# State strips in eight array tiles and two PSUM banks, scores in 64x32 tiles, rank updates in 128x32 tiles, and a new written order

## The chip, the core and the metric

The kernel runs on one core of one Trainium2 chip. The metric is the device time of one execution in microseconds (us); lower is better. The kernel before takes 317.76 us, the median of three runs (317.02 to 318.30). Its profiled execution took 317.11 us, of which the trace covers a span of 315.4 us. The engines are named as in the profile: PE is TensorE (its weight loads are PEld), DVE is VectorE, ACT is ScalarE, POOL is GpSimd, and SP issues most of the DMAs.

## The reference

A gated linear attention (4 batches, 8 heads, 768 tokens, 48 features a head) feeds a gated feed-forward layer with a convolution over three tokens:

```python
f = 1 / (1 + exp(-f_logit))
for t in range(S):                                   # S = 768
    state = f[:, :, t, :, None] * state + einsum('bhd,bhe->bhde', k[:, :, t], v[:, :, t])
    y[:, :, t] = einsum('bhd,bhde->bhe', q[:, :, t], state)
x = y.transpose(0, 2, 1, 3).reshape(B, S, H * D)     # H * D = 384
h = maximum(x @ w_in, 0)                             # 384 -> 1024
conv_out = sum over k of conv_w[k] * (h shifted by k - 1 tokens)
out = (h * sigmoid(conv_out)) @ w_out                # 1024 -> 384
```

## The kernel before, in words

The recurrence is computed in 24 chunks of 128 tokens (4 batches of 6), n = 0 to 23. Heads go in four pairs p; the two heads of a pair (j = 0, 1) lie on partitions 0 to 47 and 64 to 111. For a chunk, PE does four kinds of work, each in fp32, so that each matmul stands in the trace as two records (the transposes as one):

- **scores** (`pa`, line 330): eight matmuls of a 48x128 weight, one for each p and j, into a tile of two PSUM banks, bank j. DVE then copies the causal half into `am` (line 332).
- **values** (`py`, line 366): twelve matmuls of the running state `st` with q, and then sixteen of v with `am`, all with 32 output columns. Eight of the twelve are the 48-row "strips" (one array tile of 64 rows by 32 columns); the other four and the sixteen use all 128 rows by 32 columns. The 384 features are cut into twelve groups of 32; group g is written to column strip g % 4 and third g // 4 of one PSUM bank. ACT and DVE evacuate it as a high and a low part into `xT` (lines 393, 395).
- **turned keys** (`ptk`, line 317): four transposes of the scaled keys, evacuated into `kp`.
- **rank updates** (`pk`, line 341): eight matmuls of a 128x64 weight with v (64 columns moved), added into the state by DVE and scaled by POOL (lines 349, 351).

Heads of the pairs p = 2 and 3 are swapped between the two halves of the partitions (`half`, and the layout of the inputs), so that four strips in a row fall on four different column strips:

```python
def half(p, j):
    return 1 - j if p >= NP // 2 else j
```

The feed-forward layer works on eight half batches u of 384 tokens, once the three chunks of a half are in `xT`: `ph` (line 421, 72 matmuls a half) is x @ w_in in three single-pass products of split operands; ACT and DVE do the activation, the convolution and the gate (`hb`, `g`; lines 424 to 442); `gh` and `gl` are the split result (lines 460, 462); `po` (line 474, 24 matmuls for 128 tokens) is the product with w_out. At the start the weights are converted from float64 words by POOL, ACT and DVE (lines 175 to 191), and twelve matmuls `pz` (line 523) that nobody reads are strewn among the first chunks.

PSUM has eight banks: two for `pa` (tag A), one for `py` (tag Y), two for `ptk` and `pk` (tag s, `SB = 2`), three for `ph`, `po`, `pl` and `pz` (tag mm).

The order of the instructions is written by hand: `ORDER` is a list of tokens, each of which advances one generator by a step (`a9` scores of chunk 9, `y9` values, `s9` state, `k9` turned keys, `m2.3` a third of ph of half 2, block 3, `r0.1` part of a po, `w` one pz). Each engine executes its instructions strictly in that order and waits on semaphores where the data or a buffer isn't ready. No scheduler changes it.

Of the kernel before, what the change touches and what calls it, by code (L numbers as in the profile page):

```python
# [9 lines left out]
F32 = mybir.dt.float32  # L10
# [7 lines left out]
P = 128  # L18
# [22 lines left out]
t8 k9 F12 m1.3 m1.4 y7 P6 h1.4 m1.5 m1.4 m0.6 t9 m1.7 m1.5 s7 Q9 m1.6 p10 a8 m1.7 p10 m1.6 P6 m0.6 S1 m1.7 m0.7 y8 P4
j0.6 S2 y8 m1.1 j0.6 s8 y8 P4 m1.2 a9 K10 P7 m1.4 y8 h1.6 P6 k10 m1.2 P7 m1.7 m2.3 k10 s8 m1.6 S1 m1.5 Q10 m2.3 a9
m1.6 m2.2 r0.1 m2.4 s8 r0.0 m2.3 m1.5 m2.4 m1.4 S4 m2.4 m1.3 m2.2 P6 m2.2 m1.3 m1.2 y9 P6 j1.2 y9 M13 m1.5 P7 m1.4 s9
x12 j1.2 s10 V11 a10 L13 S4 m2.3 r0.0 j1.4 m2.5 m2.5 m1.7 G11 m2.5 m2.2 P7 r0.0 P7 P7 r0.0 j1.4 y9 p11 r0.0 r0.1 S6
h2.2 m2.4 p11 S6 r0.1 m1.6 a10 t11 F16 Q11 h2.4 S7 F17 r0.1 V12 y9 t10 S7 r0.1 s9 x12 m1.7 r0.1 K11 s9 r0.0 m1.6 r0.2
G13 m1.0 y10 m2.5 y10 m1.7 p13 m1.0 r0.1 a11 m1.1 r0.0 r0.1 m1.6 M12 m2.7 m1.1 V13 m2.7 K13 F15 j1.6 m2.7 L14 m1.0 L12
m2.0 j1.6 j1.0 V14 m2.0 r0.0 G12 m2.1 h2.6 m2.7 m2.1 m2.1 s10 p12 j1.0 m2.6 p12 m2.0 r0.2 r0.2 y10 m2.6 m2.0 m2.6 r0.2
G14 m2.2 r0.2 m2.4 h2.0 s10 m2.1 r0.2 y10 m2.5 m2.4 p13 r0.2 K12 m2.3 Q13 a11 r0.4 r0.2 m2.6 r0.4 k13 Q12 p14 k12 x15
y11 m2.2 y11 r0.5 t13 a12 m2.3 y11 t12 m2.7 r0.5 r0.4 m2.6 k13 m2.2 m2.0 r0.4 m2.3 m2.0 r0.5 y11 x15 m2.6 r0.5 m2.0
m2.4 m2.1 r0.5 K14 r0.2 m2.5 r0.2 r0.5 m2.1 m2.6 r0.4 j2.2 a12 p14 r0.4 k12 F19 m2.7 M14 G17 y12 L15 F18 s12 y12 m2.1  # L50
F20 r0.5 a13 j2.2 r0.3 m2.7 L16 m3.3 r0.4 m2.5 j2.0 r0.4 m3.2 r0.5 m3.3 h3.2 j2.4 j2.0 V16 m3.1 V15 j2.6 m3.2 y12 M15
s12 m3.2 j2.4 m3.3 m3.1 a13 m3.3 m3.1 m3.2 x18 m3.6 G15 m3.6 m3.7 G16 p15 k14 p15 y13 K15 h3.0 k14 Q15 y13 m3.1 r0.3
# [12 lines left out]
m5.4 K23 m5.6 j4.6 m5.1 m5.4 j4.6 m5.1 h5.0 m5.5 a19 h5.6 k20 m5.1 m5.5 m5.6 r2.1 m5.0 m5.0 m5.6 h5.2 m5.1 y19 m5.5
y19 p22 k21 s20 y19 s21 p22 s20 a20 r2.0 s20 Q22 r2.1 m5.1 m5.7 p23 m5.0 t22 m5.3 m5.0 m5.3 m5.1 t23 m5.3 r2.0 m5.2
m5.2 K22 m5.7 y19 m5.7 a20 m5.2 m5.7 m5.3 y20 m5.2 m5.4 m5.7 y20 m5.1 m5.6 m5.7 a21 y20 m5.4 m5.0 m5.7 r2.1 a21 r2.0
m5.5 m5.0 r2.1 m5.5 m5.0 r2.0 j5.4 s21 j5.0 m5.6 r2.1 m5.6 m5.3 j5.4 r2.1 j5.0 r2.0 r2.2 y20 r2.0 r2.2 y21 r2.0 m5.3
r2.1 y21 j5.6 M23 r2.1 a22 r2.0 V22 a22 k22 m6.6 Q23 m6.4 j5.6 m6.4 m6.6 m6.6 z m6.4 m6.6 m6.1 m5.2 m6.5 h6.4 m6.4
m5.2 m6.5 m6.4 m5.2 m6.1 h6.0 s21 m6.5 m5.3 m6.1 m6.5 m6.7 m6.1 m6.7 h6.6 k22 m6.7 j5.2 m6.2 m6.7 j5.2 m6.2 m6.1 m6.2  # L70
r2.2 m6.5 m6.3 m6.7 m6.0 y21 m6.3 m6.7 m6.2 m6.0 m6.4 r2.3 m6.3 z y21 m6.0 h6.2 r2.3 m6.2 z m6.0 y22 m6.0 m6.4 y22
m6.3 m6.1 r2.2 m6.5 s22 y22 m6.0 m6.3 a23 m6.6 m6.6 r2.3 m6.7 r2.2 m6.6 m6.3 r2.2 m6.1 m6.5 r2.2 a23 r2.2 m6.2 m6.0
r2.3 r2.5 s22 r2.3 r2.5 r2.3 m6.2 s22 r2.5 y22 r2.3 r2.2 r2.3 j6.4 y23 r2.2 j6.6 y23 j6.6 r2.5 y23 j6.0 j6.4 r2.5 r2.4
j6.0 r2.5 y23 h7.0 m6.3 m7.1 j6.2 m7.0 r2.5 m7.1 j6.2 h7.4 r2.5 m7.4 r2.4 m7.1 h7.2 m7.0 m7.1 m7.0 r3.0 m7.4 m7.0 m7.5
m7.2 m7.4 m7.5 m7.4 m7.5 m7.3 m7.5 m7.3 m7.5 m7.2 m7.1 m7.5 m7.3 h7.6 m7.1 m7.2 r3.0 m7.6 m7.2 m7.6 m7.3 z m7.6 m7.3
m7.7 m7.2 m7.3 m7.7 m7.6 m7.2 m7.7 m7.6 m7.0 r2.4 m7.7 m7.0 m7.4 r2.4 m7.6 m7.3 r3.0 m7.4 m7.1 r2.4 m7.0 m7.2 j7.0
r2.4 m7.6 j7.2 m7.4 r3.0 j7.0 r3.1 r3.0 m7.5 r2.4 m7.7 r3.1 r2.4 r3.0 m7.7 r3.1 r3.2 r3.2 r3.2 j7.4 r3.2 r3.1 m7.7
r3.2 j7.6 r3.2 r3.1 j7.2 r3.2 r3.1 r3.2 r3.2 r3.2 r3.2 r3.2 j7.6 r3.1 j7.4 r3.1 r3.2 r3.2 r3.2 r3.3 r3.2 r3.2 r3.2
r3.2 r3.0 r3.3 r3.2 r3.3 r3.2 r3.5 r3.2 r3.3 r3.0 r3.5 r3.3 r3.3 r3.5 r3.4 b r3.5 r3.3 r3.4 r3.3 r3.5 r3.4 r3.4 r3.4
r3.4 r3.5 r3.4 r3.4 r3.5 r3.5  # L80
# [4 lines left out]
def gla_moe_kernel(ctx, tc, q_in, k_in, v_in, f_in, w_in, conv_w, w_out, out):  # L85

    nc = tc.nc
    B, S, NP, _ = v_in.shape
    H = 2 * NP
    DM, DFF = w_in.shape  # L90
    D = DM // H
    HP = P // 2
    NC = S // P
    NF = DFF // P
    KT = DM // P
# [7 lines left out]
    SB = 2  # L103
# [4 lines left out]
    GAP = HP - D  # L108
# [137 lines left out]
    def half(p, j):  # L246
        return 1 - j if p >= NP // 2 else j

# [438 lines left out]
```

## Time and profile before

| | before |
|---|---|
| median of 3 runs | 317.76 us (317.02 to 318.30) |
| profiled execution | 317.11 us |
| its span | 315.4 us |
| PE busy | 307.5 us (98%), 3275 matmul records |
| PE weight loads busy | 283.4 us (90%) |
| DVE busy | 250.3 us (79%) |
| ACT busy | 225.1 us (71%) |
| POOL busy | 78.6 us (25%) |

How to read it: a busy PE says only that some matmul was under way; small matmuls in different tiles of the array overlap, and their records are longer than the distance between their starts. What a group of matmuls costs is therefore read from the chain of waits, in which a piece lasts from its first start to the next group's first start.

### The profile page before, as it was taken

The page shows a single profiled execution, that of the slowest core. Times are in us where ns is not written, and L with a number is a line of the kernel's source. Part 1 is how long each engine was busy: PE and PEld are TensorE (multiplying, and loading weights), DVE is VectorE, ACT ScalarE, POOL GpSimd, SP SyncE. Part 2 cuts the span into 40 slices and gives each one's busy share as a digit, 9 for nine tenths or more (in the row PEclk, how much of TensorE's full clock was granted, in tenths as well). Part 3 has the DMA queues.
Part 4 walks back from the last instruction along what each step waited for, and adds up shares of the span by engine and source line. Part 5 has one row for each costly group of instructions (what it writes and reads, how often), then busy time and mean ns, then how long its engine had stood idle before and what let it go on. Part 6 is the DMA issues. An engine that isn't in the chain of part 4 may idle for free.

```text
span 315.4 us, 7934 instructions
## 1 busy us (share of the span) xinstructions
PE 307.5 (98%) x3275; PEld 283.4 (90%) x3275; DVE 250.3 (79%) x363; ACT 225.1 (71%) x424; POOL 78.6 (25%) x104
## 2 busy tenths in 40 slices
PE   7899999999999999999999999999999999999995
PEld 4588988989999999999999989998999999999994
DVE  3899998999999999897858679884985596459630
ACT  5899998997898898878852995558453926576521
POOL 3547547245412150051040410064310000000000
PEclk9999999999999999999999999999999999999999
DMA  6999854691203701911174520421002001000021
GB/s 208 361 306 403 328 169 150 220 329 24 84 8 120 228 2 43 319 49 35 32 236 138 171 72 0 152 84 35 2 0 85 0 2 52 25 2 26 25 79 53
DMA packets 19370, 36.74 MB, mean 117 GB/s; under 512 B 2156, under 2 KB 5252, under 8 KB 19332
## 3 DMA queue, kind: packets, MB, share of 16 engines
q1 hardware_dynamic: 19044, 35.82, 33.4%
q8 instruction: 27, 0.44, 0.6%
q10 hardware_dynamic: 288, 0.39, 0.3%
q14 instruction: 11, 0.09, 0.1%
HBM read 31.48 MB, written 4.72 MB: 115 GB/s over the span
## 4 chain that ended last, share of the span: by engine, by line
PE 90%; DMA 3%; POOL 2%; issue 1%; ACT 1%; SPq 0%; POOLq 0%
PE ph L421 33%; PE po L474 32%; PE py L366 12%; PE pa L330 7%; DMA wis<-in_moe_w_in_dram 3%; PE pk L341 3%; PE ptk L317 2%; POOL mswi L177 1%; POOL mswi L175 1%; PE pl L283 0%; POOL st L351 0%; SPq L257 0%; POOL mscw L177 0%; POOL mscw L175 0%; ACT fb L262 0%
## 5 line engine op out<-in xcount | busy, mean ns | idle before, releaser
L421 PE MATMUL ph<-xT,wih 128*128 128x384 f32 x384 | 99.7, 340 | 0.0
L421 PEld LDWEIGHTS ph<-xT,wih 128*128 128x128 f32 x384 | 68.1, 188 | 1.7 <-ACT hb L424 0.2
L474 PE MATMUL po<-woh,gh 128*128 128x384 f32 x192 | 65.5, 341 | 0.0
L474 PE MATMUL po<-wol,gh 128*128 128x384 f32 x192 | 64.9, 338 | 0.0
L474 PE MATMUL po<-woh,gl 128*128 128x384 f32 x192 | 64.3, 335 | 0.0
L421 PE MATMUL ph<-xT,wil 128*128 128x384 f32 x192 | 64.3, 335 | 0.0
L431 DVE SCALAR_TENSOR_TENSOR g<-hb,cw,g 128x384 f32<-128x384 f32 (+1 forms) x64 | 39.2, 630 | 12.7 <-ACT g L429 12.5
L424 ACT ACTIVATE hb<-ph 128x384 f32<-128x384 f32 x64 | 30.5, 489 | 24.5 <-PE ph L421 23.8
L311 POOL TENSOR_TENSOR q<-q,fd 128x512 f32<-128x512 f32 x19 | 27.3, 1441 | 66.5 <-ACT hb L402 43.1
L462 DVE TENSOR_TENSOR gl<-g,gh 128x1024 fp32r<-128x1024 f32 (+4 forms) x34 | 34.1, 1013 | 8.4 <-ACT gh L460 8.2
L442 DVE SCALAR_TENSOR_TENSOR g<-g,hb 128x768 f32<-128x768 f32 (+1 forms) x32 | 30.6, 968 | 11.8 <-ACT g L440 11.8
L433 DVE SCALAR_TENSOR_TENSOR g<-hb,cw,g 128x384 f32<-128x384 f32 (+1 forms) x64 | 39.7, 645 | 0.1
L429 ACT ACTIVATE g<-hb,cw 128x384 f32<-128x384 f32 (+1 forms) x64 | 38.0, 615 | 2.0 <-DVE gl L462 1.7
L460 ACT CAST gh<-g 128x1024 fp32r<-128x1024 f32 (+4 forms) x34 | 26.7, 801 | 16.1 <-PE po L474 15.3
L474 PEld LDWEIGHTS po<-woh,gh 128*128 128x128 f32 x192 | 36.0, 187 | 0.8 <-issue 0.2
L474 PEld LDWEIGHTS po<-wol,gh 128*128 128x128 f32 x192 | 36.1, 188 | 0.0
L421 PEld LDWEIGHTS ph<-xT,wil 128*128 128x128 f32 x192 | 36.0, 188 | 0.0
L474 PEld LDWEIGHTS po<-woh,gl 128*128 128x128 f32 x192 | 36.0, 188 | 0.0
L332 DVE COPY_PREDICATED am<-mask,pa 128x1024 f32<-128x1024 uint8 x24 | 31.8, 1324 | 3.4 <-PE pa L330 3.3
L440 ACT ACTIVATE g<-g 128x768 f32<-128x768 f32 (+1 forms) x32 | 26.5, 849 | 10.8 <-DVE g L433 10.7
L351 POOL TENSOR_TENSOR st<-st,ft_all 128x256 f32<-128x256 f32 x16 | 15.4, 963 | 66.4 <-DVE st L349 66.4
L330 PE MATMUL pa<-q,k 48*128 48x128 f32 x384 | 27.9, 285 | 0.4 <-DVE q L311 0.4
(84 smaller groups left out, 438.1 us busy)
## 6 DMA issues: line engine op xcount, KB each, us to landing
fb<-in_f_logit_dram SPq DMA_DIRECT2D x24, 256.0 KB, 4.0
k<-in_k_dram SPq DMA_DIRECT2D x24, 256.0 KB, 4.6
q<-in_q_dram SPq DMA_DIRECT2D x24, 256.0 KB, 4.1
v<-in_v_dram SPq DMA_DIRECT2D x24, 256.0 KB, 4.7
out_dram<-ob SPq DMA_DIRECT2D x22, 192.0 KB, 1.9
wis<-in_moe_w_in_dram SPq DMA_DIRECT2D x6, 512.0 KB, 6.0
wos<-in_moe_w_out_dram SPq DMA_DIRECT2D x8, 384.0 KB, 5.4
out_dram<-ob ACTq DMA_DIRECT2D x2, 192.0 KB, 1.9
```

The lines of the kernel that those rows point to most:

```text
L311: (nc.vector if n < QV else nc.gpsimd).tensor_tensor(raw["q", n], raw["q", n], fds[n][1], ALU.mult)
L330: nc.tensor.matmul(pa[:, j, p, :], kT[r, p, :], qT[r, p, :], start=True, stop=True)
L332: nc.vector.copy_predicated(a_b[n % 2], mask, pa)
L366: nc.tensor.matmul(py[o:o + G, t, :], lhs, rhs, start=len(todo) < 4, stop=len(todo) >= total - 4)
L421: nc.tensor.matmul(ph, w, xts[b, hf][:, t, xl, :], start=(k == 0), stop=(k == 3 * KT - 1))
L424: nc.scalar.activation(hb[:, 2:HS + 2], ph, AF.Relu, scale=0.5)
L429: nc.scalar.activation(cv, hb[:, 1:n + 1], AF.Copy, scale=cw[:, 1, f:f + 1])
L431: nc.vector.scalar_tensor_tensor(cv, hb[:, 2:n + 2], cw[:, 2, f:f + 1], cv, ALU.mult, ALU.add)
L433: nc.vector.scalar_tensor_tensor(cv, hb[:, 0:n], cw[:, 0, f:f + 1], cv, ALU.mult, ALU.add)
L442: nc.vector.scalar_tensor_tensor(cv, cv, 1.0, h_b[:, fp:fp + 2, 1:n + 1], ALU.add, ALU.mult)
L462: nc.vector.tensor_tensor(lo, g[:, f:f + k], hi.bitcast(F32), ALU.subtract)
L474: nc.tensor.matmul(po, g[:, f, :], w, start=(i == 0), stop=(i == 3 * NF - 1))
```

## The change

It does five things.

1. **Layout of x.** Pair p now owns column strip p (32 partitions) in all three thirds t of the 384 features: t = 1 holds the first 32 features of head j = 0, t = 2 those of head j = 1, and t = 0 the 16 remaining ones of both. The swap of halves (`half`) goes away, and the rows of w_in and the layout of v are permuted to match outside the kernel.
2. **Values.** The tile `py` takes two PSUM banks; t = 0 and 1 lie in the first, t = 2 in the second. The sixteen products with `am` come first, then the four 128-row products with the state, and last the eight strips, which now fall on eight different tiles (two row halves by four column strips); row half 0 writes to bank 0, row half 1 to bank 1.
3. **Scores and rank updates** are cut: each 48x128 score matmul into four with 32 columns (64x32 tiles, 32 matmuls a chunk), each 128x64 rank update into two with 32 columns (128x32 tiles, 16 a chunk).
4. **`SB`** goes from 2 to 1: one PSUM bank for `ptk` and `pk`.
5. **`ORDER`** is another list (the same tokens, each as often as before).

The core of the diff (the table is cut to its first line):

```diff
-F1 F0 I0.0 L0 c M0 x1 F2 h0.4 L1 x0 I1.0 x0 M1 x1 w G0 V0 J0.0 I2.0 J0.0 w F3 p0 c G1 c L2 p0 K0 M2 J0.0 t0 Q0 J0.0
+F0 I0.0 x0 F1 x0 x1 c J0.0 L0 x1 c G0 p0 p0 K0 M0 J0.0 J0.0 Q0 J0.0 c c G1 M1 I1.0 a0 J0.0 p1 p1 J0.0 J1.0 F2 J1.0 x2 F3
...
-    SB = 2
+    SB = 1
...
         for p in range(NP):
-            for j in range(2):
-                r = slice(HP * j, HP * j + D)
-                nc.tensor.matmul(pa[:, j, p, :], kT[r, p, :], qT[r, p, :], start=True, stop=True)
+            for t in range(0, P, G):
+                for j in range(2):
+                    r = slice(HP * j, HP * j + D)
+                    nc.tensor.matmul(pa[t:t + G, j, p, :], kT[r, p, t:t + G], qT[r, p, :], start=True, stop=True)
...
             for j in range(2):
-                nc.tensor.matmul(pk[HP * j:HP * j + HP, p, :], kp[:, 2 * p + j, :], vt[:, p, j, :],
-                                 start=True, stop=True)
+                for x in (0, G):
+                    o = HP * j + x
+                    nc.tensor.matmul(pk[o:o + G, p, :], kp[:, 2 * p + j, x:x + G], vt[:, p, j, :],
+                                     start=True, stop=True)
...
-        py = ps.tile([P, KT, P], F32, tag="Y", name=f"py{n}")
+        py = ps.tile([P, NP, 2 * P], F32, tag="Y", name=f"py{n}")[:, :KT, :P]
...
+        def product(p, t, lhs, rhs, start=False, stop=False):
+            nc.tensor.matmul(py[G * p:G * p + G, t, :], lhs, rhs, start=start, stop=stop)
+
+        vt = qkv[n]
+        for t in (1, 2):
+            for p in range(NP):
+                product(p, t, vt[:, p, t - 1, :G], am[:, t - 1, p, :], start=True, stop=t == 2 and not inter)
+        for j in range(2):
+            for p in range(NP):
+                product(p, 0, vt[:, p, j, G:], am[:, j, p, :], stop=j == 1 and not inter)
+        yield
         if inter:
             st = s_b[n % 2]
             for p in range(NP):
-                for i in (0, 2):
-                    j = half(p, i // 2)
-                    r = slice(HP * j, HP * j + D)
-                    products([(3 * p + i, st[r, p, :G], qT[r, p, :])])
-            products([(3 * p + 1, st[:, p, G:], qT[:, p, :]) for p in range(NP)])
-            yield
+                product(p, 0, st[:, p, G:], qT[:, p, :])
+            for p in range(NP):
+                for t in (1, 2):
+                    r = slice(HP * (t - 1), HP * (t - 1) + D)
+                    product(p, t, st[r, p, :G], qT[r, p, :], stop=True)
+            yield
```

What the new table does to the order is seen at three places. The names in the rows: a number behind `py`, `pk`, `pa`, `ptk`, `pl`, `pz` is the chunk (or the running number of the pz), the number after `<-am` or `<-st` says which of two buffers; `ph1_7` is half 1, block 7; `po0_1` is batch 0, tokens 128 to 255; "32x128" is output columns of the weight by columns moved.

The first place is chunk 8 on PE. Before:

```order
L421 MATMUL ph1_7_1156<-xT0_1_679,wil2_1_595 128x384
L366 MATMUL py8_1185<-q8_875,st0_77 32x128 x12
L366 MATMUL py8_1185<-am0_75,v8_1109 32x128 x16
L341 MATMUL pk8_1220<-v8_1109,kp0_79 64x64 x8
L330 MATMUL pa9_1232<-q9_759,k9_914 128x128 x8
L317 MATMUL ptk10_1249<-ident_83,k10_892 128x128 x4
```

After:

```order
L362 MATMUL py8_1424<-am0_75,v8_835 32x128 x16
L340 MATMUL pk8_1442<-v8_835,kp0_79 32x64 x16
L362 MATMUL py8_1424<-q8_977,st0_77 32x128 x12
L327 MATMUL pa9_1481<-q9_1039,k9_1005 32x128 x32
L418 MATMUL ph1_6_1521<-xT0_1_814,wih_105 128x384 x2
```

The products with `am` and the rank update now stand side by side, and the strips (the last eight of the twelve) stand beside the scores of the next chunk.

The second place is PE at the start and where po of batch 0 begins. Before, the `pz` stand among the first chunks:

```order
L167 MATMUL pw_110<-am0_75 128x512 x2
L523 MATMUL pz0_137<-wih_105,woh_106 128x512
L283 MATMUL pl0_139<-tri32_88,fb0_115 128x128 x4
L523 MATMUL pz1_151<-wih_105,woh_106 128x512
L283 MATMUL pl1_161<-tri32_88,fb0_115 128x128 x4
L523 MATMUL pz2_179<-wih_105,woh_106 128x512
```

After, the start has none of them:

```order
L166 MATMUL pw_110<-am0_75 128x512 x2
L279 MATMUL pl0_134<-tri32_88,fb0_115 128x128 x4
L279 MATMUL pl1_152<-tri32_88,fb0_115 128x128 x4
L327 MATMUL pa0_160<-q0_144,k0_128 32x128 x32
L313 MATMUL ptk0_215<-ident_83,k0_128 128x128 x4
```

Ten of the twelve now stand between the first two po of batch 0 (the other two follow within the next 60 rows), of which the first two and the last are shown:

```order
L471 MATMUL po0_0_1709<-woh_106,gl0_0_1549 128x384
L520 MATMUL pz0_1743<-wih_105,woh_106 128x512
L520 MATMUL pz1_1747<-wih_105,woh_106 128x512
...
L520 MATMUL pz9_1769<-wih_105,woh_106 128x512
L471 MATMUL po0_1_1771<-woh_106,gh0_1_1578 128x384
```

The twelve matmuls have moved from the first 21 us of the program to its middle.

The third place is DVE ahead of the causal copy of chunk 10, on which the values of chunk 10 wait. Before:

```order
L462 TENSOR_TENSOR gl0_1_1280<-g0_639,gh0_1_1279 128x1024
L191 TENSOR_TENSOR wol6_1432<-wo6_1115,woh_106 128x384
L332 COPY_PREDICATED am0_75<-mask1_93,pa10_1370 128x1024
L395 TENSOR_TENSOR xT1_1_1416<-py9_1312,xT1_1_1416 128x3x128
L191 TENSOR_TENSOR wol7_1460<-wo7_1242,woh_106 128x384
L349 TENSOR_TENSOR st0_77<-pk9_1348,st1_78 128x256
L431 SCALAR_TENSOR_TENSOR g1_1142<-hb_101,cw_109,g1_1142 128x385
```

After:

```order
L190 TENSOR_TENSOR wol7_1716<-wo7_1472,woh_106 128x384
L428 SCALAR_TENSOR_TENSOR g1_1327<-hb_101,cw_109,g1_1327 128x385 x3
L348 TENSOR_TENSOR st0_77<-pk9_1629,st1_78 128x256
L459 TENSOR_TENSOR gl0_1_1579<-g0_715,gh0_1_1578 128x1024
L430 SCALAR_TENSOR_TENSOR g1_1327<-hb_101,cw_109,g1_1327 128x385 x2
...
L459 TENSOR_TENSOR gl0_2_1779<-g0_715,gh0_2_1778 128x8x127
L430 SCALAR_TENSOR_TENSOR g1_1327<-hb_101,cw_109,g1_1327 128x385
L439 SCALAR_TENSOR_TENSOR g1_1327<-g1_1327,hb_101 128x770
L303 TENSOR_TENSOR k11_1827<-k11_1827,fi11_1814 128x512
L329 COPY_PREDICATED am0_75<-mask1_93,pa10_1663 128x1024
```

Work of the feed-forward layer that stood behind the copy of chunk 10 on DVE now stands ahead of it.

## Rows read from the trace of the kernel before

**Rows 1.** Chain that ended last: start us, us, piece; its first ph and its end.

```profile
32.97 5.21 PE ph L421 x30
...
311.52 0.02 issue
```

**Rows 2.** Stretches of 20 us: us, busy (count) of PE, PEld, DVE, ACT, POOL; clock, DMA.

```profile
20.00:40.00 20.00, 19.60 (x315) 16.95 (x314) 19.88 (x28) 18.60 (x40) 10.79 (x15) 1.00 0.91 338
...
80.00:100.00 20.00, 20.00 (x212) 18.71 (x215) 19.88 (x30) 16.99 (x29) 5.55 (x6) 1.00 0.17 54
100.00:120.00 20.00, 20.00 (x218) 18.96 (x216) 19.54 (x28) 18.58 (x33) 5.41 (x5) 1.00 0.31 101
...
160.00:180.00 20.00, 20.00 (x229) 18.43 (x228) 13.14 (x18) 11.62 (x23) 5.96 (x7) 1.00 0.58 189
```

**Rows 3.** The chain around chunks 4, 8, 12 and 13, and a half of ph.

```profile
45.44 0.93 PE py L366 x24
46.37 0.61 PE pk L341 x16
47.99 1.09 PE pa L330 x16
...
76.01 1.80 PE py L366 x56
...
125.33 1.01 PE py L366 x32
...
136.73 1.08 PE pk L341 x32
...
269.44 12.70 PE ph L421 x72
```

**Rows 4.** Timeline of PE and its loads, chunk 4: start us, us, operation, count [idle before].

```profile
45.37 0.31 PE L366 MATMUL py<-q,st 48*32 48x128 f32 x4
...
45.37 0.37 PEld L366 LDWEIGHTS py<-q,st 48*32 48x32 f32 x16 [0.25 <-issue]
45.94 0.16 PEld L366 LDWEIGHTS py<-q,st 128*32 128x32 f32 x8 [0.20 <-issue]
```

**Rows 5.** Timeline of DVE at the copies of chunks 10 and 12, PE at values 10.

```profile
93.81 1.34 DVE L332 COPY_PREDICATED am<-mask,pa 128x1024 f32<-128x1024 uint8 x1
...
122.92 1.32 DVE L332 COPY_PREDICATED am<-mask,pa 128x1024 f32<-128x1024 uint8 x1
...
100.19 1.06 PE L366 MATMUL py<-am,v 128*32 128x128 f32 x32
```

**Rows 6.** DVE's groups by shape: count, busy us, mean ns, idle before.

```profile
L288 DVE TENSOR_TENSOR_SCAN fb<-going,fb 128x512 f32<-128x512 f32 x18 | 21.7, 1212 | 3.5 <-ACT fb L265 3.5
L431 DVE SCALAR_TENSOR_TENSOR g<-hb,cw,g 128x385 f32<-128x385 f32 x32 | 19.8, 638 | 10.2 <-ACT g L429 10.1
L307 DVE TENSOR_TENSOR k<-k,fi 128x512 f32<-128x512 f32 x24 | 18.6, 774 | 4.2 <-ACT fi L296 4.0
L442 DVE SCALAR_TENSOR_TENSOR g<-g,hb 128x770 f32<-128x770 f32 x16 | 15.0, 953 | 5.1 <-ACT g L440 5.1
L349 DVE TENSOR_TENSOR st<-pk,st 128x256 f32<-128x256 f32 x16 | 6.6, 413 | 3.7 <-PE pk L341 3.7
L191 DVE TENSOR_TENSOR wol<-wo,woh 128x384 fp32r<-128x384 f32 x8 | 4.4, 549 | 0.0
L462 DVE TENSOR_TENSOR gl<-g,gh 128x1016 fp32r<-128x1016 f32 x3 | 4.0, 1350 | 0.0
```

**Rows 7.** Timeline of PE: the first two groups of pl.

```profile
6.14 1.40 PE L283 MATMUL pl<-tri,fb 128*128 128x128 f32 x8
...
7.62 1.05 PE L283 MATMUL pl<-tri,fb 128*128 128x128 f32 x8
```

**Rows 8.** Line 523 (min/median/max ns, first and last start), and DVE at 30 us.

```profile
L523 PE MATMUL pz<-wih,woh x12: 387/474/1415, 4.9 to 20.3; 128*128 128x512 f32 x12
...
30.40 0.55 DVE L395 TENSOR_TENSOR xT<-py,xT 128x384 fp32r<-128x384 f32 x1
```

More of the change, by code (lines that the diff above doesn't have):

```diff
@@ L358, in values @@
         qT, am = raw["q", n], a_b[n % 2]
-        py = ps.tile([P, KT, P], F32, tag="Y", name=f"py{n}")
+        py = ps.tile([P, NP, 2 * P], F32, tag="Y", name=f"py{n}")[:, :KT, :P]
         inter = c > 0 or n == 0
-        todo = []
-        def products(items):
-            for g, lhs, rhs in items:
-                t, o = g // 4, G * (g % 4)
-                nc.tensor.matmul(py[o:o + G, t, :], lhs, rhs, start=len(todo) < 4, stop=len(todo) >= total - 4)
-                todo.append(g)
-        total = (7 if inter else 4) * NP
+        def product(p, t, lhs, rhs, start=False, stop=False):
[8 more added lines that the diff above has]
+        yield
         if inter:
@@ L372, in values @@
             for p in range(NP):
-                for i in (0, 2):
-                    j = half(p, i // 2)
-                    r = slice(HP * j, HP * j + D)
-                    products([(3 * p + i, st[r, p, :G], qT[r, p, :])])
-            products([(3 * p + 1, st[:, p, G:], qT[:, p, :]) for p in range(NP)])
-            yield
-        vt = qkv[n]
-        products([(3 * p + i, vt[:, p, half(p, j), x:x + G], am[:, half(p, j), p, :])
-                  for p in range(NP) for i, j, x in ((0, 0, 0), (1, 0, G), (2, 1, 0))]
-                 + [(3 * p + 1, vt[:, p, half(p, 1), G:], am[:, half(p, 1), p, :]) for p in range(NP)])
-        yield
+                product(p, 0, st[:, p, G:], qT[:, p, :])
[3 more added lines that the diff above has]
+                    product(p, t, st[r, p, :G], qT[r, p, :], stop=True)
+            yield
         hf = c // CPH
@@ L573, in grouped @@
                     for i in range(B * H):
-                        x = src[i // H, i % H // 2, half(i % H // 2, i % 2), t0 // P, :D, t0 % P:t0 % P + TB]
+                        x = src[i // H, i % H // 2, i % 2, t0 // P, :D, t0 % P:t0 % P + TB]
                         if nm == "f" and i // H * NC + t0 // P < PN:
-                            d0 = (i % H - i % 2 + half(i % H // 2, i % 2)) * HP
+                            d0 = i % H * HP
                             x = f_in[i // H, t0:t0 + TB, d0:d0 + D].rearrange("t d -> d t")
@@ L583, in gla_moe_kernel @@
                 for i in range(B * H):
-                    o = half(i % H // 2, i % 2) * HP
+                    o = i % 2 * HP
                     for c0, e0, n in ((0, 0, D),) if i % 2 == 0 else ((0, GAP, G), (HP - GAP, 0, GAP)):
@@ L613, in gla_moe_kernel @@
                         src = yb[b * H + h:b * H + h + 1]
-                        dst = x_d[b:b + 1, t0:t0 + TB, :]
-                        nc.sync.dma_start(dst[:, :, h * D:(h + 1) * D], src)
+                        dst = x_d[b:b + 1, t0:t0 + TB, :].rearrange("o t (k e) -> o t k e", k=KT)
+                        o = h // 2 * G
+                        for e0, n, kt, x in ((0, G, 1, o), (G, GAP, 0, o)) if h % 2 == 0 else \
+                                ((0, GAP, 0, o + GAP), (GAP, G, 2, o)):
+                            nc.sync.dma_start(dst[:, :, kt, x:x + n], src[:, :, e0:e0 + n])
             sxt = {}
@@ L647, in _laid_out @@
         z = np.zeros_like(x[..., :16])
-        x, y = np.concatenate([x, z], axis=3), np.concatenate([y[..., 16:], z, y[..., :16]], axis=3)
-        n = x.shape[2] // 2
-        a = np.concatenate([np.concatenate([x[:, :, :n], y[:, :, :n]], axis=3),
-                            np.concatenate([y[:, :, n:], x[:, :, n:]], axis=3)], axis=2)
+        a = np.concatenate([x, z, y[..., 16:], z, y[..., :16]], axis=3)
+    elif name == "moe_w_in":
+        a = a.reshape(4, 3, 32, -1)[:, [1, 0, 2]].transpose(1, 0, 2, 3).reshape(a.shape)
     elif name in ("q", "k", "f_logit"):
```

106 lines of the change are left out of this document (51 added, 55 removed).

## The prediction

> **What bounds the kernel now.** I read the chain of waits first. From the first ph to the end of the last po it is one unbroken run of PE, 32.97 to 311.52 us [rows 1]: 278.5 us in which PE waits for nothing. So a microsecond taken from PE there is worth a microsecond, up to the point where another engine is late. The stretches of 20 us tell which one that is: DVE is busy 19.9 of 20 us from 20 to 40 and from 80 to 100, 19.5 from 100 to 120, and only 13.1 between 160 and 180 [rows 2]. The timeline tells how much DVE has in hand where PE needs it: the causal copy of chunk 10 ends at 93.81 + 1.34 = 95.15 and its values start at 100.19, 5.0 us later [rows 5]; that of chunk 12 ends at 124.24 and its values start at 125.33, 1.1 us later [rows 3, 5]. PE is the bound, and DVE stands about 1 us behind it at the worst place.
>
> **What a group costs on PE.** The strips open four matmuls within 0.31 us, of 0.29 us each, so different array tiles run side by side [rows 4]. A group of one tile size runs in rounds, a round being one pass in each tile that it uses. In chunk 8, where the products with the state and with `am` follow each other, 56 records take 1.80 us. Alone, the strips take 45.94 - 45.37 = 0.57 [rows 4], the other four products 0.93 - 0.57 = 0.36, the sixteen products 1.01 [rows 3]. Without the size change between the last two they take 1.80 - 0.57 = 1.23 in place of 1.37: **a change of tile size costs 0.14 us** (the loads sit idle 0.20 us at each [rows 4], instead of being hidden). The rest is ten rounds of four (40 records): 1.09 / 10 = **0.109 us a round** of 128 columns. The strips, 16 records in tiles of four, are then 4 rounds + 0.14 = 0.57, as seen. Scores: 16 records in two tiles, 8 rounds; 1.09 us, so a change into their 128-column weights costs about 0.2. Two rank updates together take 1.08 and one 0.61 [rows 3]: 0.47 for 8 rounds of 64 columns, 0.058 a round.
>
> **The change on PE, part by part.**
> - Strips: eight different tiles in place of four twice, so 2 rounds in place of 4: 21 chunks have them, 21 x 2 x 0.109 = -4.6 us.
> - Scores: 64 records in eight tiles are again 8 rounds, of 0.109 or 0.112: -0.6 at most. Their 32-column weights make the change of size cheaper, 0.14 for 0.2: 24 x 0.06 = -1.3.
> - Rank updates: 32 records in four tiles are 8 rounds again: 0.
> - Opening a round of eight takes longer than one of four: four starts take 0.31 - 0.29 = 0.02 us [rows 4], so about 0.03 more at some 22 places: +0.6.
> - Order: in chunk 8 the sizes were 64x32, 128x32, 128x64, 64x128; now 128x32, 64x32. Counted along both orders, 115 changes become 91: 24 x 0.14 = -3.4.
>
> Sum: -9.3 us of PE work. 2.4 of these lie ahead of the first ph, where PE waits for data anyway and which I count at nothing, so 6.9 lie in the chain.
> - The twelve pz moved: they ran between 4.9 and 20.3 us [rows 8], beside waits; now they stand among the po. A pz is a single pass of 512 columns; by a ph of 384 (12.70 / 72 = 0.176 us [rows 3]) it is 0.235 at most, and I take 0.21, as a pass of 384 carries a fixed part too: 12 x 0.21 = +2.6 in the chain.
>
> From the first ph on PE has thus 278.5 - 6.9 + 2.6 = 274.2; adding up all groups of the new order with the prices above gives 274.8, which I use.
>
> At the strips, two row halves write to one PSUM bank side by side: 0.57 us for 16 records is four rounds [rows 4]. [...]
>
> **When the first ph can start.** It needs the low part of `xT` of chunk 2, which DVE wrote at 30.40 + 0.55 = 30.95 [rows 8]. PE then still had scores, a prefix sum, a rank update and a transpose in front, until 32.97. In the new order DVE has about the same work before that write (28 us by mean durations; a copy at that place in the old queue ends some 3.4 us above such a sum), so 31.5 us. PE alone would end at 31.5 + 274.8 = 306.3.
>
> **What is late next: DVE.** No DVE instruction is removed. Ahead of the copy of chunk 10 the new order has, by counting both queues: 8 more `g` of 385 (8 x 0.638), one `g` of 770 (0.953), one `gl` (1.350), one scan (1.212), one `k` (0.774), one `wol` (0.549), one `st` (0.413) [rows 6]: 10.35 us. DVE had no idle time to take that from (0.12 us between 80 and 100), so the copy would end at 95.15 + 10.35 = 105.5, or 104.7 if I correct the means by the old queue, whose sum to this copy is 1.4 us above its clock time and to the next one 3.0. Behind the values of chunk 10 PE had 311.5 - 100.2 = 211.3 us; now it has 203.2 (27 fewer ph at 0.176, 20 fewer rounds of strips, 13 fewer changes of size, cheaper ones into the scores; one chunk's rank update and one pz more). So PE can't end before 104.7 + 203.2 = 307.9. For chunk 12 DVE has 2.24 us more in front: 126.5 + 180.6 = 307.1. The second and third po of batch 0, which wait for `gl`, and the release of the value bank at chunk 10 give 307.7 to 308.4 by the same sum. The same sum over the old order gives 311.4 to 311.7 at its tightest places, where 311.5 was seen. I take 308.2: **3.3 us earlier**. The pz fall just into that stretch (around 100 us), where PE would wait for DVE; they cost nothing on top.
>
> The end follows PE by 315.4 - 311.5 = 3.9 us, and the execution its span by 317.1 - 315.4 = 1.7. The median of the runs is 0.65 above the profiled one. So 308.2 + 3.9 + 1.7 + 0.65 = 314.4 us. I call 0.5% (1.6 us) the least that a measurement tells from no change.
>
> **Bounds of what the trace doesn't show.** Eight tiles at once: best 2 rounds for the strips, worst 4, and 16 for the scores. One bank for `ptk` and `pk`: nothing, if each is evacuated before the next (the new order leaves 0.9 to 20 us between them, half of the 39 under 3.3); at worst DVE's and ACT's queues hold it, some 10 times by half a microsecond. [...]
>
> **Rivals.**
> - *DVE keeps up* (13%): with PE ahead, DVE waits less for `pa` and `ph` than before, and the PE sum decides: 306.3 + 6.25 = 312.6; if ahead of that the pz lie in waits too, 310.0. For it: DVE idled 6.3 us in the first 20. Against it: in the next 100 us there is hardly a wait left to remove.
> - *The start gives it back* (14%): a lower clock or a late load moves the first ph and the DVE queue by 3 us: 317.5, no change. For it: rows 7. Against it: the new order loads less ahead of the first ph.
> - *The single bank* (11%, slower): PE stands at `pk` or `ptk` until the previous one is read. It decides from the point where those waits sum to over 3.3 + 1.6 us; 20 of the short distances at 0.4 us are 8 us: 308.2 + 8 + 6.25 = 322.5. For it: `st` after `pk` and `kp` after `ptk` stand behind whole rows of `g` in the queues. Against it: none of the sums over DVE's queue for these places lies above 307.0.
> - *The tiles don't run eight abreast* (6%, slower): in fours the scores of 20 chunks in the chain cost 8 rounds more each, 20 x 0.87 = 17.4, and the strips keep 3.9: PE 296.1 after 31.5, so 333.9. Against it: four tiles of both row halves do run abreast, and four 128x32 tiles take in as many rows at once as eight of 64x32.
> [...]
>
> **How the numbers follow.** The forecast has 55%; its own range is 312.3 to 316.1, all of it faster. Faster is 55 + 13 = 68%, the same 14%, slower 18%. The range of 80% goes from the best PE sum, 310.0, to 319.0, which takes in the case of no change and the small end of the bank's waits.
>
> **What would show it.** Right: 21 strip groups of 2 rounds and score groups of 0.87 + 0.14 us; about 91 gaps of PE's loads; DVE at 19.5 of 20 us until 130 us, and PE waiting for DVE between 90 and 130. Wrong: score groups near 1.9 us, PE waits at `pk` or `ptk` above 1 us, a first ph after 34 us, or a DVE with idle time while PE waits for another engine.

## The result, and the profile after

The changed kernel takes 321.75 us, the median of 20 runs (318.39 to 325.17), against 317.75 us for the kernel before in the same session: a ratio of 1.0091, with a 95% interval of 1.0066 to 1.0116. Ratios, here and below, compare undisturbed executions alone, so they can lie a little beside those of the medians. The forecast was 314.4 us and faster; it is slower, and outside the range. The profiled execution took 323.8 us with a span of 322.1 us, 2 us above that median, so the places of its waits are read from it and not its total; the run e12 below shows the three early ones again, within 0.15 us, in an execution 0.7 us above its median. It has 4,747 matmul records (3,275 before), each with a weight load of its own: 9,494 PE instructions in place of 6,550.

The chain of waits of the changed kernel, its beginning, a few pieces of the middle and its end (start us, us, piece; "issue" is time in which PE waited for nothing that the profile shows):

```profile
16.50 1.42 issue
...
23.33 1.00 issue
...
27.16 0.95 PE py L362 x25
28.11 2.64 issue
30.76 0.65 PE py L362 x7
31.41 2.01 PE pl L279 x8
33.42 1.20 PE py L362 x24
34.61 1.71 PE pa L327 x64
36.32 1.43 PE pl L279 x8
...
38.19 3.13 PE ph L418 x18
...
54.53 0.73 PE ph L418 x3
...
68.07 0.99 issue
...
81.57 1.01 PE py L362 x32
82.58 0.45 PE pk L340 x32
83.03 0.60 PE py L362 x24
83.62 0.93 PE pa L327 x64
...
100.38 2.38 PE pz L520 x10
...
276.35 12.48 PE ph L418 x72
...
318.24 0.48 ACT ob L476
```

The first ph comes at 38.19 us, where the kernel before has it at 32.97 [rows 1] and the forecast 31.5. Ahead of it PE stands still three times, 1.42 + 1.00 + 2.64 = 5.06 us, each time in the middle of a group. At the longest, 25 records of a `py` are done, and the next 7 wait for no semaphore and start 2.64 us later. The kernel before has no such place. Behind the first ph there are four more (2.94 us). Chunk 8, by contrast, is about what was forecast: strips and the rest of `py` 0.60 us behind the rank update, where a size change and four strip rounds made it 0.93 [rows 3], and scores of 0.93.

Stretches of the changed kernel (us; busy us and count of PE, PEld, DVE, ACT, POOL; granted clock; DMA share, GB/s):

```profile
25.00:27.50 2.50, 1.66 (x96) 1.30 (x80) 1.83 (x3) 1.95 (x4) 1.34 (x3) 1.00 1.05 415
27.50:30.00 2.50, 0.61 (x21) 0.45 (x14) 2.50 (x5) 2.29 (x5) 0.00 (x0) 1.00 1.04 390
30.00:32.50 2.50, 1.74 (x12) 1.36 (x12) 1.75 (x4) 0.00 (x0) 2.11 (x3) 0.54 0.84 315
32.50:35.00 2.50, 2.50 (x53) 1.89 (x59) 0.00 (x0) 0.88 (x2) 1.42 (x3) 0.50 0.13 45
...
80.00:100.00 20.00, 20.00 (x385) 18.68 (x385) 19.83 (x34) 17.39 (x36) 6.49 (x7) 1.00 0.15 44
100.00:120.00 20.00, 20.00 (x246) 18.69 (x245) 19.85 (x28) 16.68 (x28) 7.42 (x8) 1.00 0.42 139
```

Near the end of the longest stall (PE busy 0.61 of 2.5 us) the granted clock falls to 0.50, for 6.8 us (30.2 to 37.0 us). Groups there cost up to nearly twice as much: `pl` 2.01 us for 1.09 in the version with whole scores below. DVE is as full from 80 to 120 as the forecast had it.

**Where PE stands still.** Counting PE's instructions along the trace, the 79 that neither load nor multiply included (73 of them wait on semaphores; 9,573 in all), the seven stalls come behind numbers 449, 705, 961, 2497, 7105, 7873 and 8385: any two are a multiple of 256 apart. The page has a DMA queue that brings instructions (packets, MB, share of 16 engines), here in the changed kernel and in the version with whole scores:

```profile
q8 instruction: 38, 0.62, 0.8%
```

```profile
q8 instruction: 29, 0.48, 0.6%
```

A transfer is 16,384 bytes (0.62 MB / 38), and 9,573 / 256 = 37.4: by these counts one for each 256 PE instructions (7,190 / 256 = 28.1 in the version with whole scores). Each stall ends 2.2 to 2.6 us after its block's transfer began (at 28.13 us for the one that ends at 30.76). So the theory to test was: **PE runs out of instructions**.

### The profile page after: what moved, and what is told of

The parts are those of the page before. It is cut to its first block, busy times and chain, and to the rows that moved or that the text cites. A ratio compares the mean times of both kernels' runs of the same rounds, so it can differ in the third digit from the quotient of the medians.

```text
span 322.1 us, 10858 instructions
## 1 busy us (share of the span) xinstructions
PE 304.5 (95%) x4747; PEld 279.4 (87%) x4747; DVE 248.7 (77%) x363; ACT 225.1 (70%) x424; POOL 75.5 (23%) x104
## 4 chain that ended last, share of the span: by engine, by line
PE 92%; issue 3%; ACT 2%; DMA 2%; DVE 0%; SPq 0%
PE ph L418 32%; PE po L471 32%; PE py L362 12%; PE pa L327 7%; PE pk L340 3%; PE ptk L313 3%; PE pl L279 2%; DMA fb<-in_f_logit_dram 2%; PE pz L520 1%; DVE am L329 0%; ACT fb L258 0%; ACT fb L261 0%; ACT fi L292 0%; ACT fd L294 0%; ACT wis L180 0%
## 5 line engine op out<-in xcount | busy, mean ns | idle before, releaser
L418 PE MATMUL ph<-xT,wih 128*128 128x384 f32 x384 | 101.3, 344 | 1.0 <-issue 1.0
L418 PEld LDWEIGHTS ph<-xT,wih 128*128 128x128 f32 x384 | 67.4, 188 | 5.2 <-issue 3.9
L421 ACT ACTIVATE hb<-ph 128x384 f32<-128x384 f32 x64 | 30.2, 490 | 22.5 <-PE ph L418 22.1
L459 DVE TENSOR_TENSOR gl<-g,gh 128x1024 fp32r<-128x1024 f32 (+4 forms) x34 | 31.4, 935 | 9.9 <-ACT gh L457 9.9
L439 DVE SCALAR_TENSOR_TENSOR g<-g,hb 128x768 f32<-128x768 f32 (+1 forms) x32 | 31.8, 1005 | 4.5 <-ACT g L437 4.2
L362 PE MATMUL py<-am,v 128*32 128x128 f32 x768 | 27.1, 276 | 5.3 <-issue 4.4
```

Of the source, the lines that this page charges most:

```text
L362: nc.tensor.matmul(py[G * p:G * p + G, t, :], lhs, rhs, start=start, stop=stop)
L418: nc.tensor.matmul(ph, w, xts[b, hf][:, t, xl, :], start=(k == 0), stop=(k == 3 * KT - 1))
L421: nc.scalar.activation(hb[:, 2:HS + 2], ph, AF.Relu, scale=0.5)
L439: nc.vector.scalar_tensor_tensor(cv, cv, 1.0, h_b[:, fp:fp + 2, 1:n + 1], ALU.add, ALU.mult)
L459: nc.vector.tensor_tensor(lo, g[:, f:f + k], hi.bitcast(F32), ALU.subtract)
```

## The experiments

Rivals were the new order or the single `s` bank making an engine wait, and the start without pz. All times are us; a ratio is against the kernel before on the same chip. First ph and end (the start of the last `ob`) are from the chain of each profile, which is a single execution.

| version | median | ratio (95%) | first ph | end |
|---|---|---|---|---|
| before | 317.75 | 1 | 32.97 | 311.54 |
| changed | 321.75 | 1.0091 (1.0066 to 1.0116) | 38.19 | 318.24 |
| e1 whole scores | 314.91 | 0.9925 (0.9892 to 0.9959) | 30.29 | 308.41 |
| e2 whole scores and rank updates | 318.43 | 1.0025 (1.0007 to 1.0042) | 30.38 | 311.77 |
| e3 before with small tiles | 321.88 | 1.0141 (1.0110 to 1.0172) | 37.11 | 314.69 |
| e4 changed, pz early | 321.58 | 1.0100 (1.0079 to 1.0120) | 35.08 | 317.86 |
| e6 scores 64x64 | 316.36 | 0.9943 (0.9917 to 0.9970) | 33.24 | 309.95 |
| e7 before with rank tiles | 315.15 | 0.9916 (0.9896 to 0.9935) | 32.75 | 309.48 |
| e8 whole scores, no pz | 316.16 | 0.9933 (0.9902 to 0.9964) | 33.00 | 310.60 |
| e10 cut from chunk 4 on | 316.29 | 0.9918 (0.9886 to 0.9950) | 33.80 | 310.53 |
| e11 64x64 from chunk 4 on | 314.63 | 0.9877 (0.9838 to 0.9917) | 31.42 | 308.12 |
| e12 cut in chunks 0 to 3 | 319.66 | 1.0031 (1.0000 to 1.0062) | 36.52 | 314.66 |
| e13 before, rank and 64x64 tiles | 314.59 | 0.9900 (0.9871 to 0.9929) | 33.90 | 309.78 |
| e14 new order alone | 322.09 | 1.0133 (1.0107 to 1.0159) | 31.59 | 316.59 |
| e15 e14 with one bank | 321.67 | 1.0141 (1.0100 to 1.0181) | 34.59 | 319.46 |

**e1: scores whole again.**

```diff
-            for t in range(0, P, G):
-                for j in range(2):
-                    ...pa[t:t + G, j, p, :], kT[r, p, t:t + G]...
+            for j in range(2):
+                ...pa[:, j, p, :], kT[r, p, :]...
```

> The changed kernel with the scores of a chunk in 8 matmuls of 64x128 again (32 in the change); everything else of the change stays. Theory A (PE runs out of instructions: the changed kernel issues 9,494 PE instructions, its scores 2,304 more than before, and stands still for 0.6 to 2.9 us at 7 places, all of them 256 instructions or a multiple apart): 7,190 PE instructions, the seven stalls together fall from 10.0 us to under 3 us, the granted clock stays at 1.0 to the end, first ph at 33 to 36 us instead of 38.2; 313 to 317 us against 321.75. Rival B (the one bank for ptk and pk, or the new order, makes PE or VectorE wait): the scores have no part in it, 320.5 to 322.5 us, with PE still held up in the same stretches. Rival C (the start without pz, cold clock): 319 to 322 us, first ph still at 37 us or later and the granted clock at 0.5 somewhere between 25 and 40 us.

The chain of e1, its start, chunk 9 and its end:

```profile
17.73 6.46 DMA v<-in_v_dram
...
25.85 1.09 PE pl L279 x8
26.94 0.73 PE py L361 x24
27.68 1.09 PE pa L326 x16
28.77 1.09 PE pl L279 x8
...
30.29 3.16 PE ph L417 x18
...
84.09 0.45 PE pk L339 x32
84.54 0.60 PE py L361 x24
85.14 1.09 PE pa L326 x16
...
308.41 0.48 ACT ob L475
```

No stall at a block's end is left, the clock is 1.0 throughout, the first ph is 7.9 us earlier (earlier than expected). Cutting the scores alone turns a gain of some 3 us into a loss of 4. The three stalls (5.06 us) and the lower clock behind the third (four groups of 2.01, 1.20, 1.71 and 1.43 us take 1.09, 0.73, 1.09 and 1.09 here: 2.35) come to 7.4, about the size of the 7.9. It is no exact sum, since e1 itself waits for a load of `v` there.

**e2: rank updates whole too.**

```diff
-                for x in (0, G):
-                    ...pk[o:o + G, p, :], kp[:, 2 * p + j, x:x + G]...
+                ...pk[HP * j:HP * j + HP, p, :], kp[:, 2 * p + j, :]...
```

> The changed kernel with the scores whole (8 of 64x128 in a chunk) and the rank updates whole too (8 of 64x64 instead of 16 of 32x64): strips, layout, one s bank and the new order stay. Theory A (instruction supply): 6,550 PE instructions as before the change, no stall inside a group of matmuls that waits for nothing; 312.5 to 316.5 us, at most 1 us from the version with only the scores whole. Rival B (one s bank or the order): 320 to 322.5 us. Rival C (start without pz): 319 to 322 us, first ph at 37 us or later.

No stall, but 3.5 us slower than e1, which the theory had not said. The chain at chunk 9 shows why:

```profile
84.86 0.61 PE pk L337 x16
85.48 0.73 PE py L359 x24
```

A rank update in 128x64 tiles between values in 128x32 costs 0.61 for 0.45, and the values behind it 0.73 for 0.60: a change of tile size on either side.

**e3: small tiles in the old order**, with both edits of the change and nothing else of it.

> The kernel before, with its order, its two s banks, its strips in three rounds and its early pz, and only the scores cut into 64x32 and the rank updates into 128x32 tiles. Theory A (instruction supply): stalls of 0.5 to 3 us that wait for nothing appear in the stretches where two or more chunks follow one another (16 to 32 us, and near chunks 12 to 15), at places a multiple of 256 PE instructions apart; 318 to 322 us against 317.75, the cut scores' own gain of some 1 us included. Rival B (order or bank): no such stall, 316 to 317.5 us. Rival C (start without pz): no change of clock here since pz stand early, 316 to 317.5 us.

Five stalls, at instructions 449, 705, 961, 1217 and 6849: in another order, with other matmuls there, again multiples of 256 apart and mostly the same numbers. The first ph is 4.1 us later than in the kernel before. The new order, the single bank and the layout are not needed for it.

**e4: pz back among the first chunks**, the twelve `w` of the table moved, of which the first two are:

```diff
-... J0.0 L0 x1 c G0 p0 p0 K0 ...
+... J0.0 L0 x1 c w G0 w p0 p0 K0 ...
```

> The changed kernel with the 12 pz put back among the first three chunks (one to four of them between groups, about where the kernel before has them) instead of behind chunk 9. Rival C (start without pz): the granted clock stays at 1.0 behind 20 us, first ph comes at 32.5 to 35 us instead of 38.2, and 2.6 to 3 us of pz leave the chain near 100 us: 314 to 318 us. Theory A (instruction supply): the seven stalls stay as many and as long (9 to 11 us together) since the small matmuls stay; the clock may hold, the pz then leave the chain near 100 us for 2.6 us: 318 to 321 us. Rival B (bank, order): 319 to 321 us without stalls at block ends.

The first ph is 3.1 us earlier and the clock holds at the start, but the time does not move (321.58, above the 318 to 321 expected): six stalls of 6.6 us together remain, for seven of 8.0, the pz no longer cover the stretch where DVE is late, and a stall of 2.18 us at 195 us is followed by a lower clock again (0.86 in the 5 us shown, 0.80 in the next 5):

```profile
195.00:200.00 5.00, 2.82 (x28) 2.33 (x15) 5.00 (x7) 0.00 (x0) 1.70 (x2) 0.86 0.01 3
```

**e5 and e9: the supply by itself.** In e1, two of the pz become bursts of small matmuls that nobody reads (m is 32 columns in the first burst, 128 in the last):

```diff
+            for _ in range(20):
+                for p in range(NP):
+                    for t in range(0, P, G):
+                        for j, o in ((0, pz), (1, pu)):
+                            r = slice(HP * j, HP * j + D)
+                            nc.tensor.matmul(o[t:t + G, p * P:p * P + m], ident[r, t:t + G], going[r, p, :m], ...)
```

> The version with whole scores (e1), in which the first and the last of the 12 pz are replaced by a burst of 640 matmuls each in the form of the cut scores (64x32 tiles, constants for operands, results unused): 2,560 PE instructions, ten blocks of 256. In the first burst each matmul streams 32 columns, in the last 128. Theory A (instruction supply): each burst stands still at every 256th PE instruction until its block is there, and the two take about the same time, 18 to 26 us, though the first has a quarter of the columns. Rival (TensorE itself sets the pace, a small matmul costs what its columns cost): the cut scores took 0.93 us for 64 records, so the last takes 20 x 0.93 = 18.6 us and the first 5 to 9 us, with no stall at block ends.

In that run every matmul took about twice its usual time (a ph 0.39 us), so its 660.07 us decides nothing.

> The same kernel as in the run with the two bursts (whole scores, first and last pz replaced by 640 small matmuls each, results unused, 32 columns streamed in the first and 128 in the last), since in that run every matmul, those of the kernel before in some of its own runs too, took about twice its usual time. Theory A (instruction supply): both bursts stand still at blocks of 256 instructions and take about the same time, 18 to 26 us each. Rival (the columns set the pace): 18.6 us for the last and 5 to 9 us for the first, no stall.

386.27 us, a ratio of 1.2144 (1.2068 to 1.2219). The chain inside the first burst, and stretches of both (columns as above):

```profile
94.17 2.32 issue
...
105.25 2.22 issue
...
109.00 1.94 issue
...
112.48 1.94 issue
...
115.96 1.94 issue
...
123.18 1.94 issue
```

```profile
100.00:105.00 5.00, 2.79 (x255) 2.65 (x256) 3.40 (x5) 0.00 (x0) 0.00 (x0) 0.50 0.01 3
```

```profile
160.00:165.00 5.00, 3.67 (x176) 3.22 (x184) 0.00 (x0) 0.00 (x0) 0.00 (x0) 0.67 0.02 7
```

The stalls of the first burst are 256 instructions apart; nine of them start between 94.17 and 123.18 us: 29.01 / 8 = 3.6 us a block, or 14 ns an instruction. The 128 matmuls of a block all start within 1.2 to 1.3 us. In the last burst, with four times the columns, nine transfers begin between 150.40 and 179.03 us: 3.6 us as well. Each burst lasted longer than expected (some 34 and 37 us for 18 to 26), since a block costs 3.6 us and not 1.8 to 2.6. DMA is nearly idle there (0.01 and 0.02), so contention is not the reason. The granted clock is 0.50 through most of the first burst (100 to 130 us), but the stalls of the changed kernel, at 1.00, have the same 2.2 to 2.6 us behind the start of a transfer (2.3 to 2.7 here). The columns do not set the pace; the supply does.

**e6: scores in 64x64 tiles**, 16 matmuls a chunk.

```diff
-            for t in range(0, P, G):
+            for t in range(0, P, HP):
...
```

> The changed kernel with the scores of a chunk in 16 matmuls of 64x64 tiles (32 of 64x32 in the change, 8 of 64x128 in e1): 8,342 PE instructions, between e1's 7,190 and the change's 9,494. Theory A (instruction supply): stalls at block ends return in the first 30 us, fewer and shorter than the change's: 1 to 5 us together; 315 to 319.5 us. Rival (the 32-column form itself is what is slow, not the number of instructions): no stall, 313.5 to 315.5 us.

Inside the range of theory A, but without the stalls that it expected: 8,342 instructions are still few enough. Behind the first ph it needs 276.7 us, 1.4 less than e1. Its later first ph comes from loads: PE waits 1.2 us longer than in e1 for the gate of chunk 1 and 1.0 us longer for the `v` that stands in e1's chain; and from 25 to 27.5 us the granted clock is 0.60, where e1 has 1.00.

**e7: the kernel before with rank tiles alone.**

```diff
-                ...pk[HP * j:HP * j + HP, p, :], kp[:, 2 * p + j, :]...
+                for x in (0, G):
+                    ...pk[HP * j + x:HP * j + x + G, p, :], kp[:, 2 * p + j, x:x + G]...
```

> The kernel before with one edit: rank updates in 128x32 tiles (16 matmuls in a chunk instead of 8). Theory of tile sizes (a rank update in tiles as large as the strips' own 128x32 goes on without a pause between the two; e3's chain had 7.75 us of pk where the kernel before has 9.07): chain of pk and py together 1 to 3 us shorter, 7,190 PE instructions, at most one stall at a block's end over 0.5 us; 315.5 to 317.5 us against 317.8. Rival (the gain of 3.5 us from e2 to e1 comes from something else in the new order): 317.5 to 319 us.

Faster than expected, 315.15 us. One rank update in its chain takes 0.45 us, two together 0.89, for 0.61 and 1.08 [rows 3]:

```profile
76.97 0.45 PE pk L343 x32
...
86.13 0.89 PE pk L343 x64
```

**e8: whole scores, no pz.**

```diff
-    WARM = 12
+    WARM = 0
```

> The version with whole scores (e1) without the 12 pz, which in e1 stand in the chain near 100 us for 3.0 us. If they fill no wait there (the prediction's term of +2.6 us is real): 311.5 to 313 us. If VectorE is what PE would wait for in that stretch anyway (the prediction's step on VectorE): 314 to 315.5 us, with PE waiting for DVE between 95 and 130 us for 2 to 3 us more than in e1. If their absence lets the clock fall: 316 us or more, with a granted clock of 0.5 near 100 to 110 us.

The pz fill a wait: without them PE's loads wait in the same stretch (90 to 110 us) for

```profile
PEld po L470 <- DVE gl L458: 1.3, 1, 1.3
PEld py L361 <- PE ph L417: 0.8, 1, 0.8
PEld ph L417 <- ACT ob L475: 0.5, 1, 0.5
```

2.6 us in all (line waited for: us, times, longest), near the 3.0 of the pz; from the first ph to the end it takes 277.6 us, only 0.5 less than e1. `gl` on DVE is late there, as forecast, and by e8's chain ACT's queue with it. The time, 316.16 us, lies above the 314 to 315.5 of this case, though the clock stays at 1.00 from 85 to 115 us. In the profile the lost time lies ahead of the first ph, 2.7 us later than e1's: `v` lands 1.2 us later, and behind that wait the clock falls, with no stall at a block's end.

```profile
22.50:25.00 2.50, 1.24 (x28) 0.97 (x16) 2.50 (x5) 1.76 (x5) 1.41 (x3) 1.00 1.03 391
25.00:27.50 2.50, 2.00 (x56) 2.03 (x60) 1.35 (x2) 2.49 (x5) 1.60 (x3) 0.58 1.05 404
```

**e10, e11 and e12: cut scores in a part of the chunks.**

```diff
+            w = G if n >= 4 else P      # e10; e11: HP if n >= 4; e12: G if n < 4
+            for t in range(0, P, w):
...
```

> The changed kernel with the scores of chunks 0 to 3 whole and those of chunks 4 to 23 in 64x32 tiles, so all cut scores stand behind the first ph. If the loss is mostly a late start (stalls ahead of the first ph and the clock that falls behind them): first ph at 30 to 33.5 us, two to four stalls of 0.6 to 1.5 us later on, 315 to 317.5 us. If the loss is in the later stalls: 318 us or more.

> As the last one, with 64x64 tiles for chunks 4 to 23. No stall at block ends as with 64x64 everywhere, PE 276.6 us from the first ph to the end as there, first ph at 30 to 33 us as with whole scores: 313 to 315.5 us. If whole scores in the first four chunks give nothing (the 3 us that lay between those two versions' starts were loads that came late in one execution): the same as with 64x64 everywhere, 315.5 to 316.5 us.

> The mirror: scores of chunks 0 to 3 in 64x32 tiles, those of chunks 4 to 23 whole. If the loss is mostly a late start: first ph at 35 to 38.5 us with two or three stalls of 1 to 3 us ahead of it, no stall later, 277 to 279 us of PE behind it: 318 to 321.5 us. If the loss is in the later stalls: 314 to 316.5 us.

Most of the loss is in the first four chunks. Cut there alone (e12), three stalls put the first ph at 36.52 us and the gain is gone; its chain, up to the first ph, has the changed kernel's pieces:

```profile
15.98 1.57 issue
...
22.96 1.00 issue
...
27.73 2.65 issue
...
36.52 3.15 PE ph L419 x18
```

Cut behind them (e10) they cost one stall of half a microsecond (0.45 us at 141 us, behind number 4,801). e11, with 64x64 tiles there, has none, and the lowest ratio of all.

**e13, e14 and e15: what the other parts are worth.** e13 is e7 with the scores of chunks 4 to 23 in 64x64 tiles (the edit of e11); e14 is the kernel before with the new table and with the two halves of `values` exchanged, as the table wants; e15 is e14 with

```diff
-    SB = 2
+    SB = 1
```

> The kernel before with rank updates in 128x32 tiles and the scores of chunks 4 to 23 in 64x64 tiles; old order, old strips, two s banks, early pz. If smaller tiles, few enough for the instruction supply, are the gain: PE from the first ph to the end some 1.1 to 1.4 us shorter than with rank tiles alone (276.6), first ph at 32 to 33.5 us, no stall at block ends over 0.5 us: 313 to 315 us. If the new order and the strips' second bank are needed for it: 315 to 316.5 us.

> The kernel before with the new order alone (values issue the products with am before those with the state, as the order wants), old strips in three rounds, whole scores and rank updates, two s banks. The step of the forecast (the order by itself takes 3.4 us of size changes off PE and adds 2.6 us of pz): 316 to 318 us. By the ledger of the version with strips, order and one bank but whole tiles (281.3 us of PE behind the first ph at 30.1; the strips there 3.7 us cheaper than these): 285 us behind 30 us, 320 to 322.5 us, so the order gains only together with tiles of one size.

> The last one with one s bank. If the single bank makes PE wait (the rival of the forecast): 1 to 8 us slower than with two, with PE waiting at ptk or pk. If each group is read before the next one comes: within 0.6 us of it.

e13 reaches e11's time without the strips' second bank, the new layout or the new order. The order alone is 1.3% slower. One bank in place of two changes nothing that these runs tell: 1.0141 and 1.0133, with 284.9 and 285.0 us behind the first ph. The later first ph of e15 (34.59) is that of a profiled execution 3.3 us above its median, in which the clock is 0.50 from 25 to 30 us.

## Why the prediction was wrong, step by step

**The step that failed** is "Scores: 64 records in eight tiles are again 8 rounds ... -0.6 at most", with 1.3 for the cheaper size change. A group's cost was counted in rounds of the array alone. The rounds were right: eight tiles do run abreast, and scores behind strips take 0.93 us for 1.09. But the cut adds 2,304 PE instructions, and the term for supplying them was missing. In the profiled executions it measured +7.9 us ahead of the first ph (stalls, and the clock that falls behind them) and +2.9 behind it, against a gain of 1.6; by the medians of e1 and the changed kernel, 6.8 us in all.

**When the first ph can start.** 31.5 us was forecast; with whole scores it is 30.3 us (e1), with the cut ones 38.2. The reckoning from DVE's queue was sound; the lacking term was what PE's instructions cost ahead of that ph. The rival "the start gives it back" named a lower clock and a first ph some 3 us late. Both came (a clock of 0.50 from 30.2 to 37.0 us), and with them the forecast's own sign of being wrong, a first ph after 34 us; but mostly from the stalls, since e1 has no early pz either and starts at 30.3 us with the clock at 1.00. That rival's rows 7 are no sign of a lower clock: the granted clock of the kernel before is 1.00 from 4 to 10 us, and what made its first `pl` group the longer one no run shows.

**PE's work.** Two runs that differ in one part price that part behind the first ph. Strips, with their layout and second bank (e15 to e2): 284.9 to 281.4, so 3.5 of 4.6. The scores' pieces of the chain fell from 21.8 to 20.2 us, so 1.6 of 1.9; in e3's old order they stay at 21.8. The sum had two slips (12 x 0.21 is 2.5, 24 x 0.06 is 1.4), each of 0.1 us; the pz cost 3.0 for 2.6. Ten of them in a row take 2.38 us (the chain above), 0.24 each; that a pass carries a fixed part, for which 0.21 was taken, was an estimate that no run shows.

"Rank updates: 0" and "Order: -3.4" were both off. The order alone (e14) takes 285.0 us behind the first ph for 278.6: +6.4, of which 3.0 are pz, so +3.4 in place of -3.4. The rank tiles then give 3.3 (e2 to e1, 281.4 to 278.1). Together the two are worth about nothing. The size changes behind the first ph did become fewer, 94 to 75, and 3.4 us cheaper in all, counted from start to start; what I didn't count is that ph now stands in 43 groups instead of 21. The first ph of a group takes 0.26 us (behind transposes) or 0.28 (behind scores) before the next one starts, those in a row 0.174: a group of three takes 0.73 us where 72 take 12.48 (the chain above). By the chain's pieces ph takes 104.5 us in place of 102.7.

**DVE next.** PE's end was to be 308.2 us because of DVE, and without the cut scores it is 308.4 (e1); its time, 314.91, is the forecast's within half a microsecond. That is partly luck, since PE's own work is longer too. The sharper test is e8: of the 3.0 us that leave PE near 100 us, 2.6 come back as waits.

**The rivals.** The single bank costs nothing (e15). Eight tiles do run abreast (scores of 64 records in 0.93 us). Of the 18% for slower, 1% stood for a least distance between the starts of matmuls, a term that no run shows: the burst's matmuls in e9, 128 with their loads in 1.3 us, start 10 ns apart. No rival was the main cause.

But the start of the new order, without pz, costs something too, in a part of the executions. In the profiles of e6, e8 and e15 the clock falls at the wait for `v`, with no stall at a block's end. Of e1's 12 executions the seven with a mean granted clock of 0.998 or more take 313.97 to 315.02 us, the five at 0.995 or less 315.56 to 317.91. The 12 of e7 and e13, which keep the old order and its early pz, are all at 0.997 or more; whether the pz alone make that difference no run shows. It is not the main loss: the two executions of the changed kernel at 0.999 and 1.000 still take 319.98 and 320.33 us.

What stays open: what decides when a block's transfer is asked for. At the three early stalls of the changed kernel it began with 57, 86 and 0 instructions of the block in hand left, and why it was not sooner no run shows. Nor does any run show why the clock falls at the start of some executions and holds in others: in e1's profile it holds though PE is busy only 0.69 us from 22.5 to 25.

## What to carry to other kernels

Price a cut of a matmul into smaller array tiles in instructions too: an fp32 matmul stands in these traces as two loads and two passes, and a long dense stretch that ate 256 instructions in less than 3.6 us stood still (e9). Cut where it makes neighbours equal in tile size (the rank updates, 2.7 us by themselves), and only as far as that needs; keep the stretches whole where several small groups follow one another and everything waits for the first large one. Read the granted clock of every execution, too: a version can look slower or faster by 3 us for where its clock fell (e1). And when a change is a bundle, look at its parts: here one cut undid the rest.

## What the hardware did that was not expected

- PE's instructions came in blocks of 256, one every 3.6 us in a stretch that only waits for them (e9), with 2.3 to 2.7 us from the start of a transfer to the next matmul (2.2 to 2.6 in the changed kernel).
- The stalls keep their instruction numbers when the program is reordered (449 in the changed kernel, e3, e4 and e12).
- The granted clock fell to 0.50 near the end of the stall of 2.64 us (PE busy 0.61 of 2.5 us) and stayed there for 6.8 us; in e4 it fell behind the stall of 2.18 us (0.86 and 0.80 in the two stretches of 5 us). In e8 it fell at the end of a wait for a load (PE busy 1.24 of 2.5 us, then 0.58 in the next 2.5).
- A row of 128x384 matmuls pays about 0.09 us at its opening behind transposes, which have the same tile size (0.26 us from the first start to the second for 0.174), and nothing behind `po` (0.174).
